# Output products by a seven-form scheme with the output matrix stationary in four column tiles, and one order list for the vector work

## The chip, the cores and the metric

The kernel runs on one core of a Trainium2 chip. The core has TensorE (PE, matrix products into the accumulator memory PSUM), VectorE (DVE), ScalarE (ACT), GpSimd (POOL, which works on the on-chip memory SBUF only), and SyncE (SP), from which most transfers are issued here. Each engine takes its instructions in the order of its own queue; semaphores order the engines among each other. The metric is device time in microseconds (us) from the first to the last instruction, the median of several runs. All numbers are float32.

## What is computed

The reference is a causal convolution over seven positions, with weights per head (192 channels in 8 heads, softmax over the seven taps), then a gated feed-forward block on 32768 tokens:

```python
# x: 8 x 4096 x 192, weight: 8 heads x 7 taps
w = softmax(weight)                       # over the taps
out = einsum('hk,bskhg->bshg', w, windows of 7 positions of x)
x = out.reshape(32768, 192)
rms = np.sqrt(np.mean(x * x, axis=-1, keepdims=True) + 1e-06)
xn = x / rms * rms_g
g = xn @ w_gate                           # 192 x 1536
silu = g * (1.0 / (1.0 + np.exp(-g)))
val = xn @ w_val                          # 192 x 1536
return silu * val @ w_out                 # 1536 x 192
```

## The kernel before

The tokens are taken in 32 pairs of two tiles of T = 512 tokens. D = 192, P = 128, FC = 12 chunks of 128 hidden features, NF = 3 chunks in a unit, NU = 4 units. The first pair goes a plain way, the other 31 the way shown here.

**Gate and value products.** Tokens are columns. A unit computes 3 chunks for both tiles with 15 products instead of 18, of sums of the weights (`wf`, made once) with sums of the inputs (`xb`, `xc`, made per pair by VectorE, 11 sums). The contraction is 64 rows long, so the gate uses the lower half of TensorE's rows and the value the upper half at the same time. The products run through six accumulators in PSUM; copies of partial states are taken on the way (by ScalarE or VectorE), and results are formed from them.

```python
# one product (act "P"): L680
nc.tensor.matmul(
    out=new(v, h, True) if first else old(v, h), lhsT=wf[u][HALF[h], WAT[i], :],
    rhs=x_op(XOP[i])[HALF[h]], start=first, stop=True, skip_group_check=True,
)
# "F", "S": copies of a bank to a bank or to a tile, on ScalarE (L689) or VectorE (L691, L693)
# "C": sum of two tiles on GpSimd (L697)
# "D", "R": bank plus or minus a tile on VectorE (L702); R gives a gate or a value
# "G": silu on ScalarE (L706)
# "M": h = value * silu(gate) (L709), on GpSimd if the value lies in SBUF, else on VectorE
e.tensor_tensor(out=hv(v), in0=src, in1=tl["g", v][:], op=ALU.mult)
# ... the order and engine of all these stand in PLAN, one list of times for a unit of 1509 ticks:
SPAN, PLAN = 1509, (
    (0, 0, "T", "P", 4, 11, ()), (100, 0, "T", "P", 1, 4, ()), (138, 1, "T", "P", 4, 11, ()),
    (142, 0, "A", "S", (4, 0), ()), (200, 0, "T", "P", 5, 6, ()),
    # ... cut
)
```

**Output products.** The hidden values `h` (128 features x 128 tokens) are stationary, the output matrix `wo_sb` moves with 192 columns, again in two halves of 64 rows: 2 tiles x 4 blocks x 12 chunks = 96 steps of two matmuls side by side. The two halves lie in two PSUM banks; ScalarE copies one and VectorE adds the other.

```python
def mm(h, bks, g, j, w, f, first, give=None):
    # ... bank choice cut
    nc.tensor.matmul(                                             # L774
        out=bank(h, bks[h])[:, w : w + D],
        lhsT=hts[f // NF][HALF[h], g, f % NF, j * P : (j + 1) * P],
        rhs=wo_sb[HALF[h], f, :], start=(f == 0 and w == 0),
        stop=(f == FC - 1), skip_group_check=True,
    )
def low(dst, bks, n):
    nc.scalar.copy(out=dst, in_=bank(0, bks[0])[:, 0:n])          # L782
def upp(dst, bks, n):
    nc.vector.tensor_tensor(out=dst, in0=bank(1, bks[1])[:, 0:n], in1=dst, op=ALU.add)  # L786
```

**Work ahead.** While the output products of pair p run, VectorE does the convolution of pair p + 2 (one `tensor_scalar`, L416, and six `scalar_tensor_tensor`, L418, of 128 x 1536), its square sums and scaling (L439 to L462), and the input sums of pair p + 1 (L608) once `xb` has been fetched from DRAM:

```python
for k in range(K):                                                # in conv(p)
    xk, w = t[:, k : k + TB, :], tp[:, k : k + 1]
    if k == 0:
        nc.vector.tensor_scalar(out=y, in0=xk, scalar1=w, scalar2=None, op0=ALU.mult)
    else:
        nc.vector.scalar_tensor_tensor(
            out=y, in0=xk, scalar=w, in1=y, op0=ALU.mult, op1=ALU.add
        )
# in x_sums(p)
for d, a, b in XSUM:
    nc.vector.tensor_tensor(out=xc[:, d, :], in0=x_op(a), in1=x_op(b), op=ALU.add)
# ... for each pair, in ticks from the start of its output products:
put(base + (LAG if p else 450), functools.partial(fetch, p + 1))
c = base + (0 if p else 200)
later(conv(p + 2), *[c + 250 + 200 * i for i in range(K)], c + 1640)
later(norm(p + 2), c + 1650, c + 1850, c + 2050, c + 2420, c + 2440)
```

At the start, GpSimd also forms the weight sums (L347, 128 x 128 each), and a transposition of the first pair's inputs runs through TensorE as full 128 x 128 matmuls (L546).

Of the kernel before, what the change touches and what calls it, by code (L numbers as in the profile page):

```python
# [19 lines left out]
def kernel(  # L20
# [22 lines left out]
    T = 512  # L43
# [45 lines left out]
    SPAN, PLAN = 1509, (  # L89
        (0, 0, "T", "P", 4, 11, ()), (100, 0, "T", "P", 1, 4, ()), (138, 1, "T", "P", 4, 11, ()),  # L90
        (142, 0, "A", "S", (4, 0), ()), (200, 0, "T", "P", 5, 6, ()),
        (238, 1, "T", "P", 1, 4, ()), (280, 0, "A", "F", 0, (1, 0), 1, ()),
        (300, 0, "T", "P", 4, 9, ()), (322, 0, "V", "S", (5, 0), ()),
        (338, 1, "T", "P", 5, 6, ()), (343, 1, "A", "S", (4, 0), ()),
        (393, 1, "V", "F", 0, (1, 0), 1, ()), (400, 0, "T", "P", 0, 8, ()),
        (414, 0, "A", "S", (4, 1), ()), (438, 1, "T", "P", 4, 9, ()),
        (477, 1, "A", "S", (5, 0), ()), (500, 0, "T", "P", 5, 13, ()),
        (538, 1, "T", "P", 0, 8, ()), (540, 0, "A", "S", (0, 0), ()),
        (600, 0, "T", "P", 4, 5, ()), (603, 1, "A", "S", (4, 1), ()),
        (629, 0, "V", "D", 5, (0, 0), 1, ((0, 0),)), (638, 1, "T", "P", 5, 13, ()),  # L100
        (666, 1, "A", "S", (0, 0), ()), (700, 0, "T", "P", 1, 10, ()),
        (700, 0, "G", "C", ("c", 3), (4, 0), (5, 0), 1, ((4, 0), (5, 0))),
        (729, 0, "A", "S", (4, 2), ()), (738, 1, "T", "P", 4, 5, ()),
        (755, 1, "V", "D", 5, (0, 0), 1, ((0, 0),)), (792, 0, "A", "S", (5, 1), ()),
        (800, 0, "T", "P", 0, 3, ()), (827, 0, "V", "R", 1, (4, 2), -1, ("b1", (4, 2))),
        (838, 1, "T", "P", 0, 3, ()), (855, 1, "A", "S", (4, 2), ()),
        (860, 1, "G", "C", ("c", 3), (4, 0), (5, 0), 1, ((4, 0), (5, 0))),
        (898, 1, "V", "S", (5, 1), ()), (900, 0, "T", "P", 4, 7, ()), (922, 0, "A", "G", 1, ()),
        (938, 1, "T", "P", 1, 10, ()), (969, 0, "V", "R", 0, (4, 1), -1, ("b0", (4, 1))),
        (1000, 0, "T", "P", 5, 2, ()), (1014, 0, "A", "F", 2, (4, 3), 1, ()),  # L110
        (1038, 1, "T", "P", 4, 7, ()), (1041, 1, "V", "R", 0, (4, 1), -1, ("b0", (4, 1))),
        (1077, 0, "A", "G", 0, ()), (1103, 0, "T", "P", 4, 12, ()),
        (1112, 1, "V", "R", 1, (4, 2), -1, ("b1", (4, 2))), (1138, 1, "T", "P", 5, 2, ()),
        (1152, 1, "A", "F", 2, (4, 3), 1, ()), (1172, 1, "G", "M", 0, ("g0",)),
        (1183, 0, "V", "F", 3, (5, 2), -1, ()), (1203, 0, "T", "P", 2, 1, ()),
        (1218, 0, "A", "S", (4, 4), ()), (1241, 1, "T", "P", 4, 12, ()),
        (1255, 1, "V", "F", 3, (5, 2), -1, ()), (1303, 0, "T", "P", 3, 14, ()),
        (1326, 0, "V", "R", 2, (5, 1), -1, ((5, 1), "b2")), (1333, 1, "G", "M", 1, ("g1",)),
        (1341, 1, "T", "P", 2, 1, ()), (1355, 1, "A", "S", (4, 4), ()),
        (1397, 0, "V", "R", 5, (4, 4), -1, ("b5", (4, 4))), (1403, 0, "T", "P", 4, 0, ()),  # L120
        (1421, 0, "A", "G", 2, ()), (1441, 1, "T", "P", 3, 14, ()),
        (1469, 1, "V", "R", 5, (4, 4), -1, ("b5", (4, 4))), (1496, 0, "A", "G", 5, ()),
        (1540, 1, "V", "R", 2, (5, 1), -1, ((5, 1), "b2")), (1541, 1, "T", "P", 4, 0, ()),
        (1571, 0, "A", "G", 4, ("b4",)), (1591, 1, "G", "M", 5, ("g5",)),
        (1611, 0, "V", "R", 3, ("c", 3), 1, (("c", 3), "b3")),
        (1683, 1, "V", "M", 4, ("b4", "g4")), (1709, 0, "A", "G", 3, ()),
        (1752, 1, "G", "M", 2, ("g2",)), (1754, 1, "V", "R", 3, ("c", 3), 1, (("c", 3), "b3")),
        (1912, 1, "G", "M", 3, ("g3",)),
# [6 lines left out]
    prods = ctx.enter_context(tc.tile_pool(name="prods", bufs=3))  # L135
# [5 lines left out]
    x_sb = {}  # L141
    TB = PT * H // P
# [21 lines left out]
    def load(p):  # L164
# [7 lines left out]
        t = x_sb[p] = xs.tile([P, NJ + HALO, D], F32, name="x_sb")  # L172
# [57 lines left out]
    few = NT - 6  # L230
    tl6 = [work.tile([P, 3, T], F32, name=f"tls{i}") for i in range(2)]
# [143 lines left out]
    def conv_first(alone=0, hot=()):  # L375
# [3 lines left out]
        for k in range(K):  # L379
# [16 lines left out]
            m = y if k == 0 else prods.tile([P, NJ, D], F32, name="m")  # L396
# [3 lines left out]
            if k in hot:  # L400
                heat(m[:].rearrange("p j d -> p (j d)")[:, 0:T], hot[k])
            if k > 0:
                nc.vector.tensor_tensor(out=y[:], in0=y[:], in1=m[:], op=ALU.add)

    def conv(p):


        if p >= PAIRS:
            return
        t = x_sb.pop(p)  # L410
        y = ys[p] = yp.tile([P, NJ, D], F32, name="y")
        y = y[:].rearrange("p j d -> p (j d)").rearrange("p (t a) -> p t a", a=GS)
        for k in range(K):
            xk, w = t[:, k : k + TB, :], tp[:, k : k + 1]
            if k == 0:
                nc.vector.tensor_scalar(out=y, in0=xk, scalar1=w, scalar2=None, op0=ALU.mult)  # L416
            else:
                nc.vector.scalar_tensor_tensor(  # L418
                    out=y, in0=xk, scalar=w, in1=y, op0=ALU.mult, op1=ALU.add
                )  # L420
            if k < K - 1:
                yield
        load(p + 1)
        yield

    yn = {}

    def norm(p):


        if p >= PAIRS:
            return
        y = ys.pop(p)[:].rearrange("p j d -> p (j d)").rearrange("p (t a) -> p t a", a=GS)
        flat = yp.tile([P, NJ * D], F32, name="yn")
        sq = flat[:].rearrange("p (t a) -> p t a", a=GS)
        nc.scalar.activation(out=sq, in_=y, func=AF.Square)
        yield
        ss = work.tile([P, TB], F32, name="s1")
        nc.vector.tensor_reduce(out=ss[:], in_=sq, axis=AX.X, op=ALU.add)  # L439
        st = work.tile([P, TB], F32, name="s2")  # L440
        nc.vector.transpose(out=st[:], in_=ss[:])
        nb = TB // Q
        r = work.tile([P, nb, NR], F32, name="r2")
        nc.vector.tensor_reduce(  # L444
            out=r[:], in_=st[:].rearrange("p (c b h) -> p c b h", c=nb, h=H), axis=AX.X, op=ALU.add
        )
        yield
        rf = r[:].rearrange("p c b -> p (c b)")
        nc.gpsimd.tensor_scalar(  # L449
            out=rf, in0=rf, scalar1=1.0 / D, scalar2=1e-6, op0=ALU.mult, op1=ALU.add  # L450
        )
        nc.gpsimd.tensor_tensor(out=rf, in0=rf, in1=nhalf[:, 0 : nb * NR], op=ALU.pow)
        yield
        wide = st[:].rearrange("p (c b h) -> p c b h", c=nb, h=H)
        for c in range(nb):
            nc.vector.tensor_copy(
                out=wide[:, c], in_=r[:, c, :].rearrange("p (b o) -> p b o", o=1).to_broadcast([P, NR, H])
            )
        nc.vector.transpose(out=ss[:], in_=st[:])
        yield  # L460
        yn[p] = flat[:].rearrange("p (a t) -> p a t", t=TB)
        nc.vector.tensor_tensor(  # L462
            out=yn[p].rearrange("p a t -> p t a"), in0=y,
            in1=ss[:].rearrange("p (t o) -> p t o", o=1).to_broadcast([P, TB, GS]), op=ALU.mult,
        )
        yield
# [22 lines left out]
    def cross():  # L489
# [17 lines left out]
        def factors():  # L507
            s2 = prods.tile([P, NJ, D], F32, name="m")
# [94 lines left out]
    def x_sums(p):  # L603
        if p >= PAIRS:
            return

        for d, a, b in XSUM:
            nc.vector.tensor_tensor(out=xc[:, d, :], in0=x_op(a), in1=x_op(b), op=ALU.add)  # L608
            yield
# [30 lines left out]
    results = {a[4] for a in PLAN if a[3] == "R"}  # L640

    def unit(u, base):


        ht = big.tile([P, 2, NF, T], F32, name="ht")
        bk, tl = {}, {}

        def hv(o):
            return ht[:, o // NF, o % NF, :]

        def new(v, h, product=False):
            bk[v, h] = pick(h, not product)
            if product:
                whole.add((h, bk[v, h]))
            assert (h, bk[v, h]) in whole
            return bank(h, bk[v, h])[:]

        def old(v, h):
            return bank(h, bk[v, h])[:]

        def grab(k):
            tl[k] = tiles.pop(0)
            return tl[k][:]

        def tile_of(t, h):

            if (t, h) in tl:
                return tl[t, h][:]
            return hv(t[0]) if h else tl["g", t[0]][:]

        def plus(s):
            return ALU.add if s > 0 else ALU.subtract
# [288 lines left out]
```

## Time and profile before

| quantity | before |
|---|---|
| time, median of 3 runs | 2722.99 us (2722.15 to 2723.37) |
| span of the profiled run | 2720.2 us, 52011 instructions |
| busy: TensorE, VectorE, ScalarE, GpSimd | 99%, 85%, 58%, 46% |
| moved by DMA | 136.78 MB, mean 50 GB/s |
| one convolution step (L418), median | 1819 ns, longest 2710 ns, 186 of them |
| one GpSimd product (L709), mean | 1305 ns |
| one VectorE result (L702), mean | 681 to 700 ns |

Busy time is the time in which an engine has at least one instruction in work; the instructions of an engine overlap a little at their ends, so that they can follow each other faster than their durations say. A matmul in float32 leaves two records of each kind, a weight load (PEld) and a matmul (PE). The releaser named with an idle time is the engine or transfer whose event came last before the instruction began.

### The profile page before, as it was taken

The page shows a single profiled execution, that of the slowest core. Times are in us where ns is not written, and L with a number is a line of the kernel's source. Part 1 is how long each engine was busy: PE and PEld are TensorE (multiplying, and loading weights), DVE is VectorE, ACT ScalarE, POOL GpSimd, SP SyncE. Part 2 cuts the span into 40 slices and gives each one's busy share as a digit, 9 for nine tenths or more (in the row PEclk, how much of TensorE's full clock was granted, in tenths as well). Part 3 has the DMA queues.
Part 4 walks back from the last instruction along what each step waited for, and adds up shares of the span by engine and source line. Part 5 has one row for each costly group of instructions (what it writes and reads, how often), then busy time and mean ns, then how long its engine had stood idle before and what let it go on. Part 6 is the DMA issues. An engine that isn't in the chain of part 4 may idle for free.

```text
span 2720.2 us, 52011 instructions
## 1 busy us (share of the span) xinstructions
PE 2687.0 (99%) x20074; PEld 2064.0 (76%) x20074; DVE 2301.5 (85%) x3282; ACT 1581.4 (58%) x2878; POOL 1262.2 (46%) x1036
## 2 busy tenths in 40 slices
PE   6999999999999999999999999999999999999999
PEld 3668888778777777776777776678877888777887
DVE  8988888888889888888888898888888888988854
ACT  5366555765556665556655556655566555566554
POOL 3854444554445544445544455444455444554433
PEclk9999999999999999999999999999999999999999
DMA  6311332122332113321223321123211233211210
GB/s 138 67 41 37 60 60 54 31 40 56 60 60 40 45 37 60 60 54 33 40 54 61 60 43 42 37 60 60 54 34 42 52 60 60 43 42 37 48 36 13
DMA packets 445080, 136.78 MB, mean 50 GB/s; under 512 B 385056, under 2 KB 419360, under 8 KB 444705
## 3 DMA queue, kind: packets, MB, share of 16 engines
q1 hardware_dynamic: 444272, 133.44, 24.6%
q8 instruction: 157, 2.57, 0.4%
q14 instruction: 91, 0.75, 0.1%
q10 hardware_dynamic: 560, 0.03, 0.0%
HBM read 83.87 MB, written 49.55 MB: 49 GB/s over the span
## 4 chain that ended last, share of the span: by engine, by line
PE 95%; POOL 1%; DVE 1%; DMA 1%; SPq 1%; issue 1%; ACT 0%; DVEq 0%; POOLq 0%
PE ps L680 59%; PE ps L774 36%; PE ps L734 1%; POOL wf L347 1%; DMA ht<-in_moe_w_gate_dram 0%; SPq L872 0%; SPq L227 0%; DMA x_sb<-in_x_dram 0%; DMA xh<-in_x_dram 0%; DVE ht L751 0%; POOL wo_sb L309 0%; DVE y L418 0%; POOL xc L308 0%; DVE xc L292 0%; DVE wf L317 0%
## 5 line engine op out<-in xcount | busy, mean ns | idle before, releaser
L680 PE MATMUL ps<-xc,wf 64*128 64x512 f32 x4960 | 1522.3, 593 | 1.4 <-DVE xc L608 1.4
L680 PEld LDWEIGHTS ps<-xc,wf 64*128 64x128 f32 x4960 | 772.8, 187 | 397.2 <-issue 186.6
L774 PE MATMUL ps<-wo_sb,ht 64*128 64x192 f32 x12288 | 1046.0, 323 | 4.2 <-DVE ht L751 2.9
L774 PEld LDWEIGHTS ps<-wo_sb,ht 64*128 64x128 f32 x12288 | 1041.3, 188 | 8.0 <-DVE ht L751 3.2
L680 PE MATMUL ps<-xb,wf 64*128 64x512 f32 x2480 | 1019.8, 590 | 0.0
L709 POOL TENSOR_TENSOR ht<-ht,tls 128x512 f32<-128x512 f32 x414 | 533.1, 1305 | 359.9 <-ACT tls L706 359.7
L680 PEld LDWEIGHTS ps<-xb,wf 64*128 64x128 f32 x2480 | 436.6, 187 | 188.7 <-issue 91.6
L689 ACT ACTIVATE tile<-ps 128x512 f32<-128x512 f32 x825 | 484.3, 596 | 140.5 <-PE ps L680 125.7
L782 ACT COPY o_sb<-ps 128x384 f32<-128x384 f32 x129 | 60.8, 471 | 793.5 <-PE ps L774 793.5
L689 ACT ACTIVATE tls<-ps 128x512 f32<-128x512 f32 x663 | 376.0, 600 | 27.8 <-PE ps L680 13.6
L418 DVE SCALAR_TENSOR_TENSOR y<-xh,tp,y 128x1536 f32<-128x1536 f32 x186 | 366.6, 1971 | 6.2
L709 POOL TENSOR_TENSOR ht<-ht,tile 128x512 f32<-128x512 f32 x206 | 267.3, 1306 | 175.7 <-ACT tile L706 175.4
L706 ACT ACTIVATE tls<-tls 128x512 f32<-128x512 f32 x414 | 255.1, 625 | 16.0 <-DVE tls L702 14.4
L702 DVE TENSOR_TENSOR ps<-ps,tls 128x512 f32<-128x512 f32 x166 | 116.1, 700 | 149.9 <-PE ps L680 149.9
L689 ACT ACTIVATE ps<-ps 128x512 f32<-128x512 f32 x372 | 216.3, 581 | 44.4 <-PE ps L680 34.3
L702 DVE TENSOR_TENSOR ht<-ps,tls 128x512 f32<-128x512 f32 x331 | 220.8, 681 | 0.0
L786 DVE TENSOR_TENSOR o_sb<-ps,o_sb 128x384 f32<-128x384 f32 x129 | 70.6, 547 | 151.0 <-PE ps L680 114.1
L702 DVE TENSOR_TENSOR ht<-ps,tile 128x512 f32<-128x512 f32 x289 | 192.3, 681 | 0.0
L449 POOL TENSOR_SCALAR r<-r 128x8 f32<-128x8 f32 x31 | 6.1, 197 | 356.0 <-DVE r L444 355.9
L702 DVE TENSOR_TENSOR tls<-ps,tile 128x512 f32<-128x512 f32 x248 | 166.8, 682 | 0.0
L691 DVE TENSOR_SCALAR ps<-ps 128x512 f32<-128x512 f32 x248 | 164.6, 695 | 0.0
L706 ACT ACTIVATE tile<-tile 128x512 f32<-128x512 f32 x206 | 127.8, 625 | 7.9 <-DVE tile L702 7.1
(105 smaller groups left out, 1945.0 us busy)
## 6 DMA issues: line engine op xcount, KB each, us to landing
xb<-xd SPq DMA_DIRECT2D x124, 384.0 KB
out_dram<-o_sb SPq DMA_DIRECT2D x63, 384.0 KB
xd<-yn SPq DMA_DIRECT2D x248, 96.0 KB
xh<-in_x_dram SPq DMA_DIRECT2D x192, 105.0 KB
xh<-in_x_dram SPq DMA_DIRECT2D x56, 98.4 KB
ht<-in_moe_w_gate_dram SPq DMA_DIRECT2D x12, 192.0 KB
ht<-in_moe_w_val_dram SPq DMA_DIRECT2D x12, 192.0 KB
tls<-in_moe_w_out_dram SPq DMA_DIRECT2D x8, 192.0 KB
```

What stands on the lines that cost most here:

```text
L347: nc.gpsimd.tensor_tensor(out=t[:, d, :], in0=t[:, a, :], in1=t[:, b, :], op=ALU.add if op == "add" else ALU.subtract,)
L418: nc.vector.scalar_tensor_tensor(out=y, in0=xk, scalar=w, in1=y, op0=ALU.mult, op1=ALU.add)
L680: nc.tensor.matmul(out=new(v, h, True) if first else old(v, h), lhsT=wf[u][HALF[h], WAT[i], :], rhs=x_op(XOP[i])[HALF[h]], start=first, st ...
L689: nc.scalar.activation(out=dst, in_=src, func=AF.Copy, scale=float(s))
L691: e.tensor_scalar(out=dst, in0=src, scalar1=-1.0, scalar2=None, op0=ALU.mult)
L702: e.tensor_tensor(out=dst, in0=src, in1=t, op=plus(s))
L706: nc.scalar.activation(out=dst, in_=src, func=AF.Silu)
L709: e.tensor_tensor(out=hv(v), in0=src, in1=tl["g", v][:], op=ALU.mult)
L734: nc.tensor.matmul(out=bank(h, bks[h])[:], lhsT=wf[u][HALF[h], k * NF + f, :], rhs=xb[HALF[h], g, k, :], start=(k == 0), stop=(k == KP - 1 ...
L774: nc.tensor.matmul(out=bank(h, bks[h])[:, w : w + D], lhsT=hts[f // NF][HALF[h], g, f % NF, j * P : (j + 1) * P], rhs=wo_sb[HALF[h], f, :] ...
L782: nc.scalar.copy(out=dst, in_=bank(0, bks[0])[:, 0:n])
L786: nc.vector.tensor_tensor(out=dst, in0=bank(1, bks[1])[:, 0:n], in1=dst, op=ALU.add)
```

## The change

Two things change for the 31 later pairs.

**Output products.** The product of `h` (1024 tokens x 1536 features) with the output matrix (1536 x 192) is seen as a product of 2 x 2 blocks and done with Strassen's scheme in Winograd's form: seven block products where eight were done, with sums before and after. The tokens are split by tile, the features by even and odd chunks, the output columns by blocks of 32. The sums of the output matrix (T1 to T4) are made once, on GpSimd. The sums of `h` (four kinds, for 6 pairs of chunks each: 24 instructions of 128 x 512 a pair) are made on GpSimd. The output matrix is now the stationary operand: 32 columns of it in each of four column tiles of TensorE, over all 128 rows, and 128 tokens move through each tile: 7 forms x 6 k x 3 blocks x 4 tiles = 504 matmuls a pair. The result lies with output columns on partitions, so VectorE transposes blocks of 32 x 32 into the output buffer (12 instructions of 128 x 128 a pair).

**Order.** PLAN, repeated for each unit, and the times of the work ahead give way to ORDER, one list for a whole pair, found by a search. `p2` stands for two TensorE steps (one matmul of a product, or one set of four column tiles); every other word is one instruction or group, with the engine in front (V, A, G, D for a transfer). C sums and products of `h` may now lie on either engine; the first convolution step is on ScalarE (`Acv0`); the end of a pair's output goes into the next pair (the words ending in `-`). Gate and value products of a step now follow each other directly, where the value was 1.38 matmuls behind.

```diff
-    SPAN, PLAN = 1509, (
-        (0, 0, "T", "P", 4, 11, ()), (100, 0, "T", "P", 1, 4, ()), (138, 1, "T", "P", 4, 11, ()),
     ... rest of the list cut
+    ORDER = (
+        "p2 Dplace- VT12- p2 AS40.0.0 AS40.1.0 p2 VF0.0.0 AF0.1.0 p2 VT22- AS50.1.0 Dst0-",
+        "VS50.0.0 p2 AS41.0.0 VS41.1.0 Acv0 GC.0.0 p2 VS00.1.0 Dst1- p2 GC.1.0 VD5.1.0",
     ... lines of the list cut (products of the four units, first h sums)
+        "AF3.0.3 p1 AS44.0.3 VC.1.3 GS3.4 p1 AS44.1.3 VR2.0.3 p1 AG1.0.3 p1 VR5.0.3 AG0.0.3",
+        "GS3.3 p1 VR5.1.3 AG4.0.3 VR3.0.3 p2 AG5.0.3 GS1.3 p1 VM0.1.3 p1 AG2.0.3 p1 VM1.1.3",
+        "p2 AG3.0.3 p1 GS2.1 Dfetch VR2.1.3 p3 Vcv3 p2 GS2.0 p6 Ac1 VM4.1.3 p3 Vcv4 p1 GS3.5",
+        "p6 GS2.3 p2 VM5.1.3 p3 VR3.1.3 p1 GS1.5 p2 As7 p1 VX3 p2 GS2.2 p1 VM3.1.3 p3 VM2.1.3",
+        "p2 GS1.4 Vcv5 p6 GS2.4 p3 VX0 p3 GS2.5 Vcv6 p6 GS4.5 p2 VX1 p1 Asq p2 VX2 GS4.0 p3",
+        "VT11 p1 Ac2 p1 Dload p1 GS4.2 Vred p6 GS4.4 p4 VX4 p1 Gpow p1 VX7 p3 VX8 p3 VX9 p3",
+        "VX6 p1 GS4.1 p4 VC22 p2 VX5 GS4.3 p3 Vbc p3 Vmul p12 VC21 p2 VX10 p3 VT21",
+    )
     ...
+    woq = wo_sb[:].rearrange("p (k two) d -> p k two d", two=2)
+    woq = woq.rearrange("p k two (m n e) -> p k two m n e", n=2, e=Q)
+    B11, B12, B21, B22 = (woq[:, :, i // 2, :, i % 2, :] for i in range(4))
     ...
+    OUTS = (
+        (1, "X", 0, 6), (7, "Z", 0, 6), (2, "Y", 0, 6), (6, "X", 0, 6), (4, "Z", 0, 3),
+        (5, "X", 0, 6), (4, "Z", 3, 6), (3, "X", 0, 6),
+    )
+    RIGHT = {1: B11, 2: B21, 3: B22, 4: T4, 5: T1, 6: T2, 7: T3}
     ...
+            for form, b, lo, hi in OUTS:
     ...
+                for k in range(lo, hi):
+                    cols = self.left(form, k).rearrange("p (b q e) -> p q b e", q=NQ, e=Q)
+                    for m in range(NM):
+                        for q in range(NQ):
+                            nc.tensor.matmul(
+                                out=self.bank(b)[q * Q : (q + 1) * Q, m * P : (m + 1) * P],
+                                lhsT=RIGHT[form][:, k, m, :], rhs=cols[:, q],
+                                start=(first and k == 0 and m == 0), stop=True,
+                                skip_group_check=True, tile_position=(0, q * Q),
+                            )
+                        yield
     ...
+        def sum(self, form, k, eng):
+            a11, a12 = self.h(0, 2 * k), self.h(0, 2 * k + 1)
+            a21, a22 = self.h(1, 2 * k), self.h(1, 2 * k + 1)
+            dst, a, b, op = {
+                1: (a21, a21, a22, ALU.add), 2: (a11, a21, a11, ALU.subtract),
+                3: (diff[k], a11, a21, ALU.subtract), 4: (a12, a12, a11, ALU.subtract),
+            }[form]
+            engine[eng].tensor_tensor(out=dst, in0=a, in1=b, op=op)
     ...
+            for m in range(NM):
+                nc.vector.transpose(
+                    out=to[:, m, n],
+                    in_=src[:, m * P : (m + 1) * P].rearrange("p (b e) -> p b e", e=Q),
+                )
     ...
+    for p in range(1, PAIRS + 1):
+        now = Pair(p) if p < PAIRS else None
+        for w in order:
+            if w[0] == "p":
+                for _ in range(int(w[1:])):
+                    if now:
+                        next(now.line)
+                continue
+            eng, name = w[0], w[1:]
     ...
```

In the list `GS2.1` is the h sum of kind 2 for k = 1 on GpSimd, `GM` and `VM` the products giving `h`, `VX3` an input sum, `Vcv3` a convolution step, `VR` a result, `VT` three transposes. Forms 7, 6, 5 and 3 read h sums of kinds 3, 2, 1 and 4; the sums of kinds 1, 2 and 4 overwrite `h`, so those of kind 2 come after form 1 has read what they replace, and those of kind 4 after form 2. The six sums of kind 3 go to a buffer of their own.

## The prediction

> **What bounds the kernel now.** I read the busy totals first, then the costliest groups, then busy time by stage, then single instructions where two engines meet.
>
> ```profile
> PE 2687.0 (99%) x20074; PEld 2064.0 (76%) x20074; DVE 2301.5 (85%) x3282; ACT 1581.4 (58%) x2878; POOL 1262.2 (46%) x1036
> ...
> PE 95%; POOL 1%; DVE 1%; DMA 1%; SPq 1%; issue 1%; ACT 0%; DVEq 0%; POOLq 0%
> ...
> L680 PE MATMUL ps<-xc,wf 64*128 64x512 f32 x4960 | 1522.3, 593 | 1.4 <-DVE xc L608 1.4
> ...
> L774 PE MATMUL ps<-wo_sb,ht 64*128 64x192 f32 x12288 | 1046.0, 323 | 4.2 <-DVE ht L751 2.9
> ```
>
> TensorE is the bound: 99% busy, 95% of the chain that ended last, and almost no idle time before either matmul group. Line 680 is the gate and value products, line 774 the output products. Each float32 matmul leaves two records: 31 pairs of 120 products are 3720 matmuls, and line 680 has 4960 + 2480 = 7440 records.
>
> The chain in order of time shows the same piece every 83.0 us (its line 680 pieces begin at 973.62, 1056.65, 1139.66), so a pair of tiles takes 83.0 us. Busy time of the two stages of one pair (columns: us, then busy us of PE, PEld, DVE, ACT, POOL, then clock and DMA):
>
> ```profile
> 641.37:692.30 50.93, 50.93 (x240) 33.13 (x238) 42.65 (x69) 44.44 (x82) 31.23 (x25) 1.00 0.04 12
> 692.30:724.60 32.30, 32.30 (x392) 32.30 (x390) 28.85 (x33) 4.95 (x9) 6.84 (x5) 1.00 0.57 105
> ```
>
> The reader is to see that GpSimd (POOL) works in the first stage and is almost free in the second, while VectorE (DVE) does its long convolution there. So about 51.6 us are products and 31.4 us output products; the cut of the window lies a little early.
>
> The last view is the timeline where the two engines meet, and one later convolution step for comparison:
>
> ```profile
> 1026.80 1.16 DVE L416 TENSOR_SCALAR y<-xh,tp 128x1536 f32<-128x1536 f32 x1
> 1027.99 2.71 DVE L418 SCALAR_TENSOR_TENSOR y<-xh,tp,y 128x1536 f32<-128x1536 f32 x1
> ...
> 1027.10 1.98 POOL L709 TENSOR_TENSOR ht<-ht,tile 128x512 f32<-128x512 f32 x1
> ...
> 1030.74 1.82 DVE L418 SCALAR_TENSOR_TENSOR y<-xh,tp,y 128x1536 f32<-128x1536 f32 x1
> ...
> 50.38 2.01 DVE L418 SCALAR_TENSOR_TENSOR y<-xh,tp,y 128x1536 f32<-128x1536 f32 x1
> ...
> 50.73 1.97 POOL L347 TENSOR_TENSOR wf<-wf 128x128 f32<-128x128 f32 x1
> ```
>
> The convolution step on line 418 takes 1.82 us alone, but 2.71 us where it starts during a GpSimd sum: 0.89 us more, close to the 1.09 us that the sum still had to run (it ends at 1029.08). That sum took 1.98 us, its neighbours 1.27; it had begun under line 416. In the start, a 128x128 GpSimd sum that takes 0.45 us alone takes 1.97: it lasts until 52.70, just past the end of the convolution step at 52.39. So these two kinds of instruction do not run side by side; one waits for the other, in both directions. VectorE instructions with one operand in PSUM are not touched: line 702 has a median of 682 ns with GpSimd busy and 681 without.
>
> **What the skill says.** "GPSIMD Engine Reference", Key points: GpSimd shares its SBUF interfaces with VectorE, with contention against VectorE instructions with two SBUF inputs or in a two-port mode. The lines above agree (0.89 us of delay). "TensorE: Matmul & The Clock Gate", Part 3, says that matmuls in different column tiles run concurrently, and gives 2.38 times for three column tiles; no run so far shows column tiles. The same part says that matmuls start strictly in order. The trace differs for row tiles: the two halves each keep their own spacing of 0.43 us and interleave, so the second record of one half starts after the first record of the other half's next matmul. That matters, because four column tiles of two records each would run only two wide if starts were strictly in order. "TensorEngine Tiling (Array Packing)", Key Properties: a change of tiling mode drains the engine; no run here shows its cost.
>
> **TensorE after the change.** The 96 steps of 192 columns in two row halves become 7 forms x 6 k x 3 blocks = 126 steps of 128 columns in four column tiles. A float32 record of 128 columns follows the next at 0.11 us in the start (line 546: 32.73, then 32.84), so two records are 0.223 us and 126 steps are 28.1 us, if the four tiles run side by side. That removes 31.4 - 28.1 = 3.3 us a pair; less 0.5 us, my estimate for two changes of tiling, 2.8 us. TensorE alone would need 80.2 us a pair.
>
> **VectorE.** I count the order list. There are 40 results, 8 D sums, 10 copies to tiles, 4 forks, 11 products and 2 C sums: 75 instructions of 512 columns. They follow each other at 0.598 us in the trace: 44.9 us. The 11 X sums take 6.6, six convolution steps at 1.854 apart 11.1, reductions 2.2, factors 0.7, scaling 2.7, two corner sums 0.9, and twelve block transposes at about 0.35 (estimate from 0.28 for half the size) 4.1. Sum 73 us, against 71.4 busy now. It fits 80 us, with little room: from the end of the products on, some 27.6 us of it lie in a 28.1 us stage, and its last piece (X sum 10) is an operand of the next pair's second product.
>
> **GpSimd.** 13 products, 6 C sums and 24 new h sums: 43 x 1.23 us + 2.3 for the power = 55 us a pair, against 38 now. By itself that fits too.
>
> **Both on the shared port.** What may not run beside a GpSimd sum is, on VectorE: the convolution 11.1, X sums 6.6, scaling 2.7, seven products with both inputs in SBUF 4.2, two C sums 1.2, together 25.8 us. 25.8 + 55 = 81 us in a pair of 80. Worse is where they lie. After the last product the list has about 17 h sums and the power on GpSimd (some 21 us) and 21 such VectorE instructions (convolution 7.4, X sums 6.6, five products 3.0, scaling 2.7: 19.7 us), plus about 8 us of VectorE work that can lie beside GpSimd.
>
> I go through the two queues by hand, alternating as the start does. The last products' results keep VectorE until 53 us; then most of the five products, four convolution steps, eleven X sums and the scaling find a GpSimd sum before them. The sixth difference (GS3.5) ends near 62 instead of 58, the last GS2 near 74 instead of 66, the last GS4 near 89 instead of 76, and X sum 10 near 92 instead of 79.6. In short: 19.7 + 21 = 40.7 us in turn, from 51.6, with starts and ends that overlap by about 0.1 us a turn. TensorE waits at form 7, at form 6, at form 3 and then at the next pair's second product. The period becomes about 91 to 95 us; I take 92.
>
> **Sum.** 31 pairs x (92 - 83) = +279 us. The end grows by about 5 us (two transposes and whole-tile stores after the last product), the start by a few. 2723 + 279 + 5 = 3007; I say 3000.
>
> **Rivals.** (1) The list holds as written: the sums slip beside VectorE with little delay. Then the period is 80 to 81.5 us and the time 2723 - 31 x 1.5 to 3 + 5, so 2635 to 2680. For it speaks that the list spaces its h sums evenly, one for every six steps of TensorE (6 x 0.22 = 1.3 us), as if nothing delayed them; against it, all the overlaps above. (2) The four column tiles run only two wide, or the short weight loads and matmuls (16 instructions in 0.22 us against 8 in 0.325 now) cannot be issued fast enough. The stage would take about 54 us, the period 105, the time near 3400. For it: nothing before runs column tiles. Against: row tiles show independent queues, and line 546 shows weight loads hidden behind matmuls of 128 columns. (3) The contention is milder because GpSimd gets ahead during the products: the period is 84 to 88 and the time 2760 to 2880. (4) TensorE's waits of up to 4 us lower its clock, which can halve (0.50 granted from 26 to 32 us of the start, 1.00 from 32.2 to 36); that adds to the main case up to 3 us a pair, 3100.
>
> **Range and chances.** Main case with (4) about 0.62, centred on 3000; (3) 0.10; (1) 0.17; (2) 0.11. A range from 2700 to 3160 holds the main case, the milder one, and small parts of the others. Faster by over 2% (below 2668.5) needs (1) nearly whole: 0.14. Within 2%: 0.13. Slower: 0.73.
>
> **What would show it.** Right: h sums on GpSimd whose mean is well above 1.3 us or that begin only as convolution steps end; convolution steps longer than 1.82 us; idle time before the output matmuls, released by GpSimd; a wait of the products for xc; TensorE far under 99%. The column steps at 0.22 us where nothing holds them would show the TensorE term right. Wrong: a period near 80 us with TensorE still at 98% (rival 1), or output records without gaps but spaced twice as far (rival 2).

## The result and the profile after

| quantity | before | after |
|---|---|---|
| time, median | 2722.65 us (4 runs, 2722.15 to 2723.37) | 3020.12 us (4 runs, 3018.61 to 3021.66) |
| ratio after to before | | 1.109, 95% interval 1.107 to 1.111 |
| span of the profiled run | 2720.2 us | 3016.8 us |
| one pair of tiles | 83.0 us | 92.65 us (products begin at 798.82, then at 891.47) |

The change makes the kernel 297 us slower. All of it lies in the 31 pairs: 31 x (92.65 - 83.0) = 299 us, by the pair shown; the others take about as long, 92.8 us on average.

The page of the changed kernel, its busy totals, the transfers of instructions, the shares of the chain that ended last, and three of the costliest groups (out and in, count, then busy us and the mean ns of one, then idle time before). L845 is an h sum, L417 a convolution step:

```profile
PE 2741.1 (91%) x39418; PEld 1883.3 (62%) x39418; DVE 2802.2 (93%) x3655; ACT 1648.5 (55%) x3061; POOL 2226.0 (74%) x1513
...
q8 instruction: 308, 5.05, 0.7%
...
PE 55%; DVE 32%; issue 8%; POOL 2%; DMA 1%; ACT 1%; SPq 1%; DVEq 0%; ACTq 0%; POOLq 0%
...
L845 POOL TENSOR_TENSOR ht<-ht 128x512 f32<-128x512 f32 x558 | 996.0, 1806 | 9.7
...
L817 PE MATMUL ps<-ht,wo_sb 128*32 128x128 f32 x13392 | 419.5, 280 | 69.5 <-DVE nt L863 27.1
...
L417 DVE SCALAR_TENSOR_TENSOR y<-xh,tp,y 128x1536 f32<-128x1536 f32 x186 | 427.0, 2296 | 0.2
```

TensorE fell from 95% of the chain to 55%, and VectorE took 32%. No engine has too much work by itself, but an h sum that should take 1.23 us has a mean of 1.81 (of the 558 that overwrite `h`), and a convolution step 2.30 where 1.82 is its time alone. The loads of TensorE's instructions (q8) have doubled, from 157 blocks to 308. That line will matter later; before, it read:

```profile
q8 instruction: 157, 2.57, 0.4%
```

Busy time by stage of one pair (columns: us, then busy us of PE, PEld, DVE, ACT, POOL, then clock and DMA):

```profile
798.80:850.30 51.50, 51.48 (x236) 29.33 (x236) 46.74 (x71) 45.23 (x86) 34.51 (x26) 1.00 0.11 29
850.30:891.50 41.20, 32.07 (x1016) 27.63 (x1014) 40.98 (x43) 6.18 (x10) 34.83 (x20) 1.00 0.38 66
```

The products keep their 51.5 us. The whole loss is in the second stage, 41.2 us, in which VectorE is busy for 40.98 and TensorE for 32.07. The chain in order of time over this stage (start, us, what):

```profile
798.82 51.49 PE ps L699 x226
...
851.01 3.52 DVE ht L745 x2
...
866.78 2.75 DVE y L417
869.53 1.68 DVE xc L622
...
873.87 3.46 DVE xc L622 x2
...
890.22 1.21 DVE o_sb L833 x6
...
891.47 1.55 PE ps L699 x5
```

From the last product of one pair to the first products of the next, the chain runs through VectorE: products of `h` (L745), convolution steps, X sums (L622, the input sums), transposes (L833). A product or an X sum that meets an h sum takes 1.7 us there and a convolution step up to 2.75, where they take 0.6 and 1.8 with nothing beside them. The timeline of the same stretch shows what is beside it (start, us, what, count):

```profile
869.45 1.75 DVE L622 TENSOR_TENSOR xc<-xb 128x512 f32<-128x512 f32 x1
871.13 2.82 DVE L417 SCALAR_TENSOR_TENSOR y<-xh,tp,y 128x1536 f32<-128x1536 f32 x1
...
861.14 18.57 POOL L845 TENSOR_TENSOR ht<-ht 128x512 f32<-128x512 f32 x10
...
860.29 1.80 PE L817 MATMUL ps<-early,x 128*32 128x128 f32 x57 [2.45 <-issue]
...
891.47 1.13 PE L699 MATMUL ps<-xc,wf 64*128 64x512 f32 x4 [0.67 <-DVE o_sb L833]
```

The ten h sums behind each other take 1.86 us each, beside eight VectorE instructions with two inputs in SBUF: nearly one sum, one VectorE instruction, one sum. TensorE's own idle times in this stretch are 0.39, 2.45, 1.47, 0.40, 0.81, 0.68, 1.75, 0.45 and 0.67 us, 9.1 in all. VectorE released 4.7 of it, GpSimd 1.2, ScalarE 0.7. The 2.45 us have no releaser ("issue"). That is a wait of another kind, and the experiments from 4 on find it.

### The profile page after: what moved, and what is told of

The parts are those of the page before. It is cut to its first block, busy times and chain, and to the rows that moved or that the text cites. A ratio compares the mean times of both kernels' runs of the same rounds, so it can differ in the third digit from the quotient of the medians.

```text
span 3016.8 us, 91662 instructions
## 1 busy us (share of the span) xinstructions
PE 2741.1 (91%) x39418; PEld 1883.3 (62%) x39418; DVE 2802.2 (93%) x3655; ACT 1648.5 (55%) x3061; POOL 2226.0 (74%) x1513
## 3 DMA queue, kind: packets, MB, share of 16 engines
q8 instruction: 308, 5.05, 0.7%
## 4 chain that ended last, share of the span: by engine, by line
PE 55%; DVE 32%; issue 8%; POOL 2%; DMA 1%; ACT 1%; SPq 1%; DVEq 0%; ACTq 0%; POOLq 0%
PE ps L699 52%; DVE xc L622 9%; DVE ht L745 8%; DVE y L417 6%; PE ps L817 2%; DVE o_sb L833 2%; DVE s L440 2%; DVE s L454 1%; DVE ht L725 1%; POOL ht L845 1%; PE ps L913 1%; POOL wf L346 1%; ACT tls L738 1%; DVE nt L863 0%; DVE tile L863 0%
## 5 line engine op out<-in xcount | busy, mean ns | idle before, releaser
L845 POOL TENSOR_TENSOR ht<-ht 128x512 f32<-128x512 f32 x558 | 996.0, 1806 | 9.7
L699 PE MATMUL ps<-xb,wf 64*128 64x512 f32 x2480 | 751.3, 595 | 0.0
L817 PE MATMUL ps<-ht,wo_sb 128*32 128x128 f32 x13392 | 419.5, 280 | 69.5 <-DVE nt L863 27.1
L660 ACT ACTIVATE tile<-ps 128x512 f32<-128x512 f32 (+1 forms) x508 | 297.1, 599 | 330.4 <-PE ps L699 316.3
L817 PEld LDWEIGHTS ps<-ht,wo_sb 128*32 128x32 f32 x13392 | 381.4, 113 | 118.1 <-POOL r L449 46.9
L660 ACT ACTIVATE ps<-ps 128x512 f32<-128x512 f32 (+1 forms) x651 | 349.2, 579 | 190.7 <-PE ps L817 87.6
L817 PE MATMUL ps<-ht,x 128*32 128x128 f32 x13392 | 392.3, 274 | 54.1 <-POOL ht L845 37.8
L417 DVE SCALAR_TENSOR_TENSOR y<-xh,tp,y 128x1536 f32<-128x1536 f32 x186 | 427.0, 2296 | 0.2
L817 PEld LDWEIGHTS ps<-ht,x 128*32 128x32 f32 x13392 | 365.9, 110 | 75.4 <-POOL ht L845 51.7
L745 POOL TENSOR_TENSOR ht<-ht,tile 128x512 f32<-128x512 f32 x195 | 251.2, 1299 | 214.3 <-ACT tile L738 214.3
L745 POOL TENSOR_TENSOR ht<-ht,tls 128x512 f32<-128x512 f32 x145 | 194.0, 1338 | 147.5 <-ACT tls L738 147.5
L845 POOL TENSOR_TENSOR early<-ht 128x512 f32<-128x512 f32 x186 | 290.6, 1578 | 0.0
L817 PE MATMUL ps<-early,x 128*32 128x128 f32 x4464 | 154.0, 287 | 84.7 <-issue 56.0
```

The costliest lines, as they stand in the source:

```text
L417: nc.vector.scalar_tensor_tensor(out=y, in0=xk, scalar=w, in1=y, op0=ALU.mult, op1=ALU.add)
L660: nc.scalar.activation(out=dst, in_=src, func=AF.Copy, scale=float(s))
L699: nc.tensor.matmul(out=self.new(v, h, True) if first else self.old(v, h), lhsT=wf[self.u][HALF[h], WAT[i], :], rhs=x_op(XOP[i])[HALF[h]], ...
L745: engine[eng].tensor_tensor(out=self.hv(v), in0=src, in1=t[:], op=ALU.mult)
L817: nc.tensor.matmul(out=self.bank(b)[q * Q : (q + 1) * Q, m * P : (m + 1) * P], lhsT=RIGHT[form][:, k, m, :], rhs=cols[:, q], start=(first ...
L845: engine[eng].tensor_tensor(out=dst, in0=a, in1=b, op=op)
```

## Theories

**The port.** An h sum on GpSimd and a VectorE instruction with two inputs in SBUF exclude each other; the turns of the two queues after the last product set the period. **Rival, duration.** GpSimd is too slow in itself: its sums hold up the forms, port or no port. **Rival, load.** VectorE has too much to do, whoever adds. **Rival, TensorE.** The column tiles or their instructions take longer than the 28.1 us assumed, and the sums are beside the point.

Each run below is one execution beside one of the kernel before on the same chip, which took 2723.4 to 2725.0 us. "Period" is the distance between the starts of the same stage in two pairs.

## Experiment 1: all h sums on VectorE

```diff
+    order = ["V" + w[1:] if w[:2] == "GS" else w for w in order]
```

> All 24 h sums of a pair go from GpSimd to VectorE, at the same places of the order list. Port theory (GpSimd sums and VectorE instructions with two SBUF inputs take turns, and these turns set the 92.6 us period): a sum costs VectorE 0.6 us, and the turns vanish but for the products and C sums of h left on GpSimd; VectorE then has 73 + 24 x 0.6 = 87.5 us of work and becomes the bound, period 88 to 91, time 2870 to 2970. Load theory (VectorE simply has too much work in this order, the port costs nothing): 14 us more work, period near 107, time near 3460. Duration theory (the h sums come late because GpSimd takes 1.23 us for each and has a queue of them): the sums come sooner, VectorE's 87.5 us bound it, like the port theory.

Measured: 3111 us. No forecast was met. The 558 sums on VectorE that overwrite `h` have a mean of 739 ns (the other 186 have 1079), so they are cheap without GpSimd beside them. But VectorE executes in order, and a sum that waits for its `h` or for form 1 holds back the results behind it. Its chain at the end of a pair:

```profile
999.28 2.50 DVE xc L622 x4
...
1002.90 5.80 PE ps L817 x144
```

Form 3 on TensorE (144 records) starts only at 1002.90, when VectorE has got through X sums and an h sum to the corner sum (`VC22`, which adds two partial results of an output block) that frees its bank. So this experiment trades one queue for another. It doesn't tell the theories apart.

## Experiment 2: only the 15 late sums on VectorE

Those from `GS2.1` on stand after the last product and need not wait long.

```diff
+    late = order.index("GS2.1")
+    order[late:] = ["V" + w[1:] if w[:2] == "GS" else w for w in order[late:]]
```

> Only the 15 h sums from GS2.1 on (those that lie in the stage of the output products) go to VectorE; the 9 early ones stay on GpSimd, where VectorE mostly works from PSUM. Port theory: VectorE 73 + 15 x 0.6 = 82 us, few turns left, period 83 to 86, time 2720 to 2820. Load theory: 9 us more, period near 102, time near 3300.

Measured: 2936 us. Both missed again. What I had left out is simple: VectorE has some 27.6 us of work of its own in the second stage (the prediction's figure), and 15 sums at 0.60 us put 9.0 beside it. 51.5 + 36.6 = 88.1 us a pair is over the 83.0 of before without a single turn. (2936 - 2723) / 31 = 6.9 us more a pair were measured, 89.9; the 1.8 us between were not traced further. So VectorE alone with these sums is too slow as well, by less, and the run says little about the port.

## Experiment 3: the 15 late sums replaced by copies on ScalarE

Two copies, 624 ns each, stand for each late sum; the addition is left out. ScalarE is almost free in this stage (6.18 of 41.2 us), and two copies take as long as a GpSimd sum alone, 1.25 us.

```diff
+            if eng == "A":
+                copy("A", dst, a)
+                copy("A", dst, b)
+                return
     ...
+    late = order.index("GS2.1")
+    order[late:] = ["A" + w[1:] if w[:2] == "GS" else w for w in order[late:]]
```

> The same 15 late h sums are each replaced by two copies on ScalarE, which read the same two tiles and write the same tile; the addition is left out. Two copies take ScalarE about 1.1 to 1.2 us, as long as a sum takes GpSimd by itself, and ScalarE has only some 6 us of other work in this stage. Port theory: no turns with VectorE any more, TensorE's 78.5 to 79 us bound it or VectorE's 73 to 75 with some waits, period 79 to 82, time 2600 to 2700. Duration theory: the sums come no sooner than GpSimd would bring them by itself; if that is what cost the time, the period stays above 88 and the time above 2880. Load theory: VectorE has the same work, the time stays near 3020.

Measured: 2819 us. A 1.25 us stand-in for each sum, on an engine off the port, takes away 201 of the 297 us. The duration of a sum therefore cannot be what costs these 201 us, and neither can VectorE's load. But the port theory said 2600 to 2700, and some 120 us too many remain. Something else waits.

## Experiment 4: no h sums at all

```diff
+    order = [w for w in order if w[:2] != "GS"]
```

The forms then read `h` where a sum of it should be (form 7 reads the buffer of its sums, which they no longer fill). Nothing else changes.

> All 24 h sums are left out; everything else, all seven forms included, stays. Port theory: nothing is left that takes turns with the convolution, input sums and scaling but the power and a few products; TensorE bounds it, period 79 to 81, time 2590 to 2670. If column tiles, the changes of tiling or the order list themselves cost time, it stays above 2720.

Measured: 2812 us, only 7 below experiment 3, so the copies had cost next to nothing, and the rest is not in the sums. TensorE's timeline at the start of a pair's column steps, this stage with its granted clock (columns as above), the largest of TensorE's waits (us in total, times, longest), and the transfers of instruction blocks, first from 1058 to 1083 us and then from 1083 to 1091 (blocks, MB, share):

```profile
1057.74 4.14 PE L817 MATMUL ps<-ht,wo_sb 128*32 128x128 f32 x144
1061.69 1.80 PE L817 MATMUL ps<-early,x 128*32 128x128 f32 x57
1066.11 3.65 PE L817 MATMUL ps<-early,x 128*32 128x128 f32 x84 [2.61 <-issue]
```

```profile
1057.74:1090.95 33.21, 30.00 (x1010) 29.25 (x1009) 25.97 (x37) 4.77 (x8) 2.46 (x2) 0.95 0.47 77
```

```profile
PE ps L817 <- issue: 107.1, 86, 4.7
```

```profile
q8 instruction: 5, 0.08, 1.4%
...
q8 instruction: 3, 0.05, 2.3%
```

TensorE stops in the middle of form 7 with nothing to wait for that the profile shows, and in the whole run it does so 86 times among the column steps, for 107 us. What it lacks is instructions, as the q8 lines suggest and experiment 7 bears out. A block is 16 KB (5.05 MB / 308 on the page of the changed kernel), and TensorE's records there are 2 x 39418 = 78836, 256 for each of the 308 blocks (before: 2 x 20074 / 157 = 256 too). So these are TensorE's own instructions, and a block holds 128 weight loads and 128 matmuls, 16 column steps. Sixteen steps at 0.218 us, the spacing where nothing holds them, need 3.5 us. While `xb` and `xh` are fetched, blocks begin to arrive at 1063.35, 1067.22, 1071.24, 1075.99 and 1080.45 us, 3.9 to 4.8 us apart; without these transfers, at 1083.91, 1087.38 and 1090.74, they are 3.4 to 3.5 apart. The two longest pauses of this stage each end shortly after a block has landed (landed at 1064.60, TensorE on at 1066.11; landed at 1081.41, on at 1082.73).

A pause can cost more than its own length. The granted clock was 0.50 from 1067.4 to 1070.6, right after the pause of 2.61 us, and the steps took 0.427 us each there. The clock was that low for 51 us of the part of the run in which the pairs lie, in 11 of the pairs. Why the clock was lowered is not shown.

## Experiment 5: eight plain forms

No Strassen scheme at all: 144 steps of column tiles, no h sums, no corner sums. The words left in the list are spread over the longer stage. (One block of `h` is read before its new value is made.)

```diff
-            for form, b, lo, hi in OUTS:
+            for g, n, b in ((0, 0, "X"), (0, 1, "Y"), (1, 0, "Z"), (1, 1, "W")):
     ...
+                for f in range(FC):
+                    cols = self.h(g, f).rearrange("p (b q e) -> p q b e", q=NQ, e=Q)
+                    right = ((B11, B12), (B21, B22))[f % 2][n]
     ...
+        elif w[:2] != "GS" and w not in gone:
+            words.append((at if at <= 120 else 120 + (at - 120) * 8 / 7, w))
```

> Column tiles and the order list stay, the seven-form scheme goes: eight plain forms, 144 steps of four column tiles for 126, no h sums, no corner sums. Every output is computed. By step counts TensorE needs 51.5 + 144 x 0.2145 = 82.4 us a pair. If the new scheme had no wait of its own: period 82.5 to 83.5, time 2710 to 2750, no gain over the kernel before. Instruction theory (column tiles need 16 TensorE instructions each 0.21 us, 2304 a pair here; they are fetched in blocks of 256, and the blocks come late while the transfers of the next inputs run, which shows as waits of TensorE for nothing the profile shows): 3 to 6 us a pair more, time 2800 to 2900.

Measured: 2947 us, above both. Its chain is TensorE and nothing else:

```profile
1013.68 7.76 PE ps L817 x277
1021.45 4.06 issue
...
1043.21 3.70 PE ps L817 x128
...
1047.22 3.70 PE ps L817 x128
...
1054.49 45.72 PE ps L700 x202
```

Near the end come 128 records and a pause, every 4.02 us (1043.21, 1047.22, 1051.24), and before them a stall of 4.06 us. This stage takes 40.8 us (1013.68 to 1054.49) where the old form took 31.4; over the run it is less, (2947 - 2723) / 31 = 7.2 us more a pair in all. So with these transfers running, column tiles cost some 7 us a pair more than the row tiles they replace, without one h sum. At 0.218 us a step, the 144 steps would take 31.4 us, no longer than the old form: an estimate from the spacing in experiment 7 below, not run.

## Experiment 6: the pieces by themselves

A kernel that computes nothing of the reference: ten GpSimd sums of 128 x 512, and groups of instructions on other engines, alone and together, with all engines brought to the same point in between.

```diff
+    sums(10); cut(); vec(20, True); cut()          # GpSimd sums; VectorE, both inputs in SBUF
+    sums(10), vec(20, True); cut()                 # together
+    sums(10), vec(20, False); cut()                # one VectorE input in PSUM
+    step(6); cut(); sums(10), step(6); cut()       # convolution steps
+    copies(20); cut(); sums(10), copies(20); cut() # VectorE copies in SBUF
+    sums(10), turns(40); cut(); sums(10), scalars(20); cut()
+    tiles(200); cut(); loads(), tiles(200); cut()  # column steps without and with transfers
```

> Pieces measured by themselves, between barriers; the convolution and the feed-forward block are left out. Sections in order: 10 GpSimd sums of 128x512 alone; 20 VectorE sums with two SBUF inputs alone; both together; 10 GpSimd sums with 20 VectorE sums that have one PSUM input; 6 convolution-like steps (128x1536) alone; the same with 10 GpSimd sums; 20 VectorE copies SBUF to SBUF alone; the same with 10 sums; 10 sums with 40 block transposes; 10 sums with 20 ScalarE copies; 200 steps of four column tiles alone; the same with 6.3 MB of loads in 2 KB pieces. Port theory: together = sum of both (about 12.3 + 12 = 24 us; 12.3 + 11 = 23 us for the steps), with a PSUM input and with ScalarE the longer of the two. Instruction theory: 0.2145 us a step alone (43 us), clearly more under the loads (over 47 us). If column tiles do not care about loads, both are the same.

The timeline (start, us, what, count; the first VectorE line holds the 20 alone and the 20 together):

```profile
9.71 13.32 POOL L42 TENSOR_TENSOR gc<-ga,gb 128x512 f32<-128x512 f32 x10 [9.27 <-SPq L85]
23.19 38.55 DVE L46 TENSOR_TENSOR vc<-va,vb 128x512 f32<-128x512 f32 x40 [13.67 <-SPq L85]
...
61.91 13.36 POOL L42 TENSOR_TENSOR gc<-ga,gb 128x512 f32<-128x512 f32 x10 [7.25 <-SPq L85]
...
87.75 21.68 POOL L42 TENSOR_TENSOR gc<-ga,gb 128x512 f32<-128x512 f32 x10 [12.48 <-SPq L85]
...
187.85 3.43 PEld L71 LDWEIGHTS pm<-va,ga 128*32 128x32 f32 x128 [0.15 <-issue]
191.58 3.43 PEld L71 LDWEIGHTS pm<-va,ga 128*32 128x32 f32 x128 [0.30 <-issue]
...
242.08 3.70 PE L71 MATMUL pm<-va,ga 128*32 128x128 f32 x128 [1.40 <-issue]
```

The table is read off that timeline:

| beside ten GpSimd sums (13.32 us alone) | sums take | both done after |
|---|---|---|
| 20 VectorE sums, both inputs in SBUF (some 14 us alone) | 16.78 us | 23.9 us |
| 20 VectorE sums, one input in PSUM | 13.36 us | 14.5 us |
| 6 convolution steps (some 11.1 us alone) | 21.68 us | 21.7 us |
| 20 VectorE copies, SBUF to SBUF (9.3 us alone) | 14.11 us | 18.5 us |
| 40 block transposes of 128 x 128 | 13.35 us | 13.8 us |
| 20 ScalarE copies | 13.39 us | 14.4 us |

Two-input VectorE work and GpSimd sums come close to adding up (23.9 of 27.3 us; 21.7 of 24.4). With one operand in PSUM, with transposes and with ScalarE they lie beside each other entirely. "GPSIMD Engine Reference", Specifications, of the Trainium skill names exactly the kinds that contend, those with two SBUF inputs or in a two-port mode; the measured sizes agree with it and go nearly as far as taking turns. The copies have one input; that they ran in such a mode is not shown. The last three lines of the timeline are the instruction supply: a block of 128 weight loads every 3.73 us (187.85 to 191.58) without any transfer, and every 4.0 to 5.1 us with transfers. The 200 steps take 46.9 us alone, where 43 were expected, and 54.6 with the transfers.

## Experiments 7, 8 and 9: the supply with and without transfers

**7** is experiment 4 without the transfers of the next inputs into `xb` and `xh`: the kernel takes the same old data again. **8** makes the same cut with all h sums on GpSimd, as the change has them. **9** is experiment 4 with all transfers, but `xb` has two buffers, and its fetch stands in the list in the second unit of the products, where TensorE needs an eighth of the instructions in the same time; in the trace it is issued earlier still, 6.1 us after the products begin (1053.5, then 1059.6). Room for it comes from `early`, two buffers for three.

```diff
 # 7 and 8 (8 keeps the words GS)
-            x_sb.pop(p)
+            x_last[0] = x_sb.pop(p)
-                    fetch(p + 1) if act == "fetch" else x_sum(int(act[1:]), eng)
+                    scr.pop(p + 1) if act == "fetch" else x_sum(int(act[1:]), eng)
-                load(p + 3)
+                x_sb[p + 3] = x_last[0]
 # 9
-    xb = cst.tile([P, 2, KP, T], F32, name="xb")
+    xbs = [cst.tile([P, 2, KP, T], F32, name=f"xb{i}") for i in range(2)]
+    order.remove("Dfetch")
+    order.insert(order.index("GM2.1.0"), "Dfetch")
```

> As the run without h sums, and besides the transfers of the next pair's inputs from DRAM (into xb and xh) are left out for the 31 pairs; the instructions that read them stay and read old data. Instruction theory: TensorE's waits of 1 to 5 us in the third form vanish, the steps run at 0.2145 to 0.22 us, period 79.5 to 82, time 2610 to 2690. If the waits have another cause (PSUM banks, order, clock), the time stays at 2780 to 2815.

> The changed kernel with its h sums on GpSimd, but without the transfers of the next inputs into xb and xh in the 31 pairs (the instructions that read them stay and read old data). If the turns at the port are a chain of their own, about 40 us long after the last product, and the late instruction blocks only lie beside it, the time hardly falls: period 91 to 92.6, time 2960 to 3020. If the two waits add up, about 4.5 us a pair go: time 2860 to 2900.

> The run without h sums, with two buffers for xb: the transfer of the next pair's xb starts at the second unit of the products, where TensorE needs few instructions, and not after the last product. All transfers are made; xh is still loaded during the output products. Instruction theory: the waits of 1 to 5 us in the third form go, period 82 to 84, time 2680 to 2750. If xb's transfer was not what delayed the instruction blocks: 2790 to 2815, as before it.

Measured: 2666 us for 7, 3021 for 8, 2705 for 9. TensorE's timeline of 7, three forms in a row, pieces of its chain around them, and the timeline of 9:

```profile
1090.35 4.14 PE L818 MATMUL ps<-ht,wo_sb 128*32 128x128 f32 x144
1094.31 4.11 PE L818 MATMUL ps<-early,x 128*32 128x128 f32 x144
1098.24 4.11 PE L818 MATMUL ps<-ht,wo_sb 128*32 128x128 f32 x144
```

```profile
1009.44 26.77 PE ps L818 x969
...
1037.54 52.88 PE ps L700 x232
1090.42 21.80 PE ps L818 x792
```

```profile
1106.37 4.14 PE L823 MATMUL ps<-ht,wo_sb 128*32 128x128 f32 x144
1110.33 4.11 PE L823 MATMUL ps<-early,x 128*32 128x128 f32 x144
...
1127.77 3.37 PE L823 MATMUL ps<-ht,x 128*32 128x128 f32 x116 [0.61 <-issue]
```

Without transfers, the pauses are gone: forms of 18 steps follow at 3.93 us (1094.31 to 1098.24), 0.218 us a step, 27.5 us for the seven. The period is 80.9 us on average of two pairs (column steps begin at 1009.37, 1090.35 and 1171.10). The first block of instructions in these two stages begins to arrive 2.7 and 3.0 us after the first column step (1012.10 and 1093.34); in experiment 4 it was 5.6 us (1063.35). With `xb` fetched early, the first forms run like that and pauses of 0.4 to 1.1 us remain near the end; the period is 82.3 (column steps begin at 1024.05 and 1106.37). So the transfers into `xb` and `xh` slow the instruction blocks, and moving one of them brings back 107 of the 146 us that both cost. Of the 146, some 105 are TensorE's waits for nothing shown (107.1 us in experiment 4, 2.4 in 7), and some 25 are an estimate for the lowered clock (half of the 51 us; in experiment 7 the clock stays at 1.00 through the pairs); the rest was not traced. How one transfer delays the other was not tried.

Run 8 settles how the two waits add: not at all. With every h sum on GpSimd and no transfers, the time is the same as with them (3021 and 3020). The turns are the longer of two chains that lie beside each other.

## Why the prediction came out right, and where it was off

The prediction was 3000 us, and 3020 was measured. By its steps:

**TensorE alone, right in sum.** It was put at 28.1 us for the 126 steps, 0.5 for two changes of tiling, and a period of 80.2. Where nothing holds the steps (experiment 7) they take 27.5 us, the stage with its changes of tiling 28.1, and the period is 80.9. The products take 52.9 us there (1037.54 to 1090.42) where 51.6 was put. So 1.3 us too few stood against 0.5 too many, and that the sum is only 0.7 off is partly luck. What the 1.3 us are was not traced. Four column tiles of two records each do run four wide, as assumed from the row tiles. "TensorE: Matmul & The Clock Gate", Part 3, says that column tiles run at the same time; 0.218 us for eight records agrees: at the 0.11 us from record to record of line 546, that is the time of two, so four run at once.

**VectorE and GpSimd by themselves, right.** 73 us of VectorE work were counted; in experiment 4 VectorE is busy for 74.2 in a pair (1057.74 to 1143.98). GpSimd was put at 55 with the sums; without them it is busy for 28.2, and 24 sums at 1.23 make it 57.7. In the changed kernel the same 3655 instructions keep it busy for 2802 us, in experiment 4 for 2395. The 408 us between are not work: they are the same VectorE instructions, longer beside h sums and counted as busy all the while.

**The turns, right in mechanism and size.** They were worth 92 - 80.2 = 11.8 us a pair on paper. Runs 8 and 7 differ by the h sums alone, with the late blocks out of the way: (3021 - 2666) / 31 = 11.5 us. These hold all that the h sums cost, their mere duration too; experiment 3, with stand-ins as long as the sums, bounds that part at (2819 - 2666) / 31 = 4.9 us, and the late blocks explain most of it. The steps by hand, counted from the start of a pair's products (798.82): GS3.5 was put at 62 and ended at 62.3, the last GS2 at 74 and ended at 73.5; the last GS4 was put at 89 and ended at 87.1 (885.94); X sum 10 was put at 92 and ended at 91.4 (890.22). One sum in it was wrong: 17 h sums of 1.23 us and the power's 2.3 make 23.2 us and not "some 21". This did no harm, since the power took no turns: X sums followed each other at 0.6 us beside it (880.04 to 883.13).

**The end of a pair, slightly wrong.** X sum 10 was named as what the next products wait for. In the trace it is what stands right behind it in VectorE's queue: six transposes (890.14 to 891.42) that free the banks. That is 1.2 us more, which the hand count had not put on the path. The estimate of 0.35 us for a transpose was too high (0.275 measured), but they come three at a time. TensorE's waits were named at form 7, form 6, form 3 and the next pair's products. Those at form 6 are there (0.40 and 0.81 us, for h sums) and so is that at form 3 (1.75 us, for a corner sum in VectorE's queue). The 2.45 us at form 7 are not for a sum in this pair; over the run form 7 waits 84.7 us, 28.7 for its sums and 56.0 for nothing shown. The waits of forms 1 and 2 for products of `h` (0.39 and 1.47 us) were not named.

**Start and end, slightly wrong.** They were to add 5 us. The pairs alone make 299 us of a difference of 297, so start and end added next to nothing.

**Rival 1, the list as written.** It fell: the sums did not slip beside VectorE. **Rival 3, milder contention.** It fell too. **Rival 4, the clock.** It plays almost no part in the changed kernel: the mean granted clock went from 0.997 to 0.983, and both stages above show 1.00. In experiment 4 it shows (0.95 in the stage above).

**Rival 2, half right, and the miss that matters.** I wrote it as one case: two wide, or too many instructions. "Two wide" is wrong. "Cannot be issued fast enough" is right in kind, though not as an issue rate of the engine: the instructions arrive too late from memory while other transfers run. In size it was far off: the stage takes 33.2 us in experiment 4 (1057.74 to 1090.95), not about 54. By itself it would have made the new kernel slower than the old one, 2812 against 2723. I had no view of it, because busy time doesn't show an engine that has no instructions; the q8 line of the page does, with 157 blocks before, and I didn't multiply. 126 steps of 16 instructions are 2016 in 28 us, against 768 in 31.4 before, and that multiplication was mine to make.

**Where the gain went.** From the top: the column steps without waits, transfers of the next inputs and h sums would give 57 us (2723 to 2666). The transfers take back 146, most of it by holding up instruction blocks (2666 to 2812). The turns add 208 more (to 3020), or 355 if they are put on first (2666 to 3021), because they hide the late blocks.

**Is there a version that beats the old one?** None of these runs is it. The best that fetches everything is 2705 us (experiment 9), without any h sum: 0.7% under the kernel before. Keeping the 24 sums costs either turns (11.5 us a pair, on GpSimd) or VectorE's time in a stage that is already full (15 sums, 9.0 us), so by these numbers no split of the 15 late sums between the two keeps that 0.7%. (The nine sums before the last product cost little: experiment 3 keeps them on GpSimd and is 7 us over experiment 4, both with the late blocks, which may hide a part.) That is argued, not run.

## What to carry to other kernels

Before work is put on a half-idle engine, ask what the two engines share: a GpSimd sum beside a VectorE instruction with two SBUF inputs saves little, beside one with a PSUM operand all of it, and busy time alone will count the wait as work. When a change cuts matmuls into smaller ones, multiply out the instructions per microsecond, and look at which transfers run in that stage. And when a change carries two possible waits, take each away alone and both together: here the longer one hid the other entirely.

## What the runs showed of the hardware that was not expected

- TensorE's instructions come in blocks of 16 KB, 256 instructions. By itself a block takes 3.73 us in a long run of column steps (0.233 us a step). With transfers into SBUF beside it, it takes 4.0 to 5.1. Before the first pause of that run, some 99 steps go at 0.218 us each (166.22 to 187.85), and so do all 126 of a pair in experiment 7.
- A column step (weights of 32 columns in each of four column tiles) takes 16 instructions for 512 tokens x 32 columns of result, since each of its four float32 matmuls leaves two weight loads and two matmuls.
- SBUF-to-SBUF copies on VectorE also contend with GpSimd sums: 20 copies and ten sums end after 18.5 us, 9.3 and 13.3 alone. The wait falls on the copy, which takes 1.37 us beside a sum and 0.43 alone; the sum takes 1.32 for 1.26. Transposes of 128 x 128 do not.
- Busy time of VectorE rises by 17% (2802 for 2395 us) with the same instructions, once the h sums run on GpSimd beside them.
